# Joining a unit's row maxima at the start of a step, and storing 18 units' maxima transposed by element-wise DMAs

## The chip, the cores and the metric

The kernel runs on one core of one Trainium2 chip. A core has a matrix engine (TensorE, PE in the profile, with its weight loads shown as PEld), a vector engine (VectorE, DVE), a scalar engine (ScalarE, ACT), a general engine (GpSimd, POOL), and a queue engine (SyncE, SP) that here does nothing but issue DMAs. The engines run side by side, each through its own instructions in program order, and wait for one another by semaphores. The metric is the device time of one execution in microseconds (us); lower is better.

## The reference

The input x has 2048 tokens of 512 features. It is normalised (layernorm without weights), and two branches read the result. One is an attention with 32 heads of 16 features; the other is an MLP with a hidden width of 1376. The output is x plus the attention's result times the silu of the MLP's result.

```
xn = layernorm(x)
q, k, v = split(xn @ wqkv)                      # 32 heads of 16
p = softmax(q @ k.T / 4, over the keys)
s = concat_heads(p @ v) @ wo
g = silu(gelu(xn @ w1 + b1) @ w2 + b2)
out = x + s * g
```

The softmax needs, for every query and head, the largest score over the 2048 keys. It is subtracted before the exponential. The change is about how these maxima get from the engine that finds them to the place where they are subtracted.

## The kernel before

The attention is cut into 32 units. A unit is 4 heads times 512 queries: `GH = 4`, `CH = 512`, so `NU = 32`. A unit is worked on twice.

First the maxima. The scores are computed with queries on the 128 partitions ("S tiles", line 185): 64 tiles of 128 queries by 512 keys for a unit. For each tile VectorE takes the maxima of its two halves (`s_max`, line 191) into the unit's tile `mx`. When all 64 are done, `s_end0` joins them: one `tensor_reduce` (line 249) turns 128x128 numbers into 128x16, negated, the tile `nm` (16 is 4 heads times 4 blocks of 128 queries). GpSimd splits it into a high and a low part, the tile `nmh` (`two`, lines 252 and 253). These two are put off to the next "X" place of the order below.

Second the exponentials. The scores are computed again, transposed, with the keys on the partitions ("T tiles", line 713, four for every block of 128 keys, one a head). The negated maxima are two more rows of the query operand `qt`, which the matmul adds to the scores, so that ScalarE can take the exponential of a T tile straight from PSUM (line 715). The probabilities times the values are summed by TensorE into `pv` (line 778); at a unit's end VectorE copies `pv` to `os` (line 785), and DMAs carry it on (`o_move`, `o_den`).

For that second pass the maxima must stand as rows, with the queries along the free side, and not spread over partitions as `nm` has them. In the kernel before, this turn is made by TensorE. `s_end1` (line 269) multiplies `nmh` by an identity into a PSUM tile, which it takes from the same ring of four banks that the T tiles use (`t_tile`); `s_end2` copies it to `mh` (VectorE, line 279; ScalarE, line 277, in the first stage) and stores it by one DMA to the DRAM tensor `mh_d` (line 280). Later `load_mh` (line 153) reads it into the rows of `qt`. The units below `PAIRED = 28` share this step two by two: `nmh` holds 64 columns, and the step is made once for units 0 and 1, once for 2 and 3, and so on, some `tick`s after the second unit of the pair has ended (`later`, `flush`).

The order of all this is written out by hand. In a first stage (up to about 465 us) the MLP and the projections fill TensorE, and the S tiles of units 0 to 8 are put between them by `fill`. Then comes the main loop, 512 steps of 16 per unit, numbered n; `ka` is the step's place in its unit. A step has the four T tiles of one block of 128 keys, the `pv` matmuls of the step before, and three S tiles for later units:

```
ORDER = {0: "TTTTV", 3: "TSXTTSTYV"}
AFTER = {0: "STXTTSTYV", 2: "XTSTTYSTV"}
```

T is one T tile with its exponential, S an S tile with its reduce, X and Y are the halves of a third S tile, V the four groups of `pv` matmuls. Each V also counts `later` down and calls `flush`. With three of 64 tiles a step, a unit of maxima takes 21.3 steps, while a unit of exponentials takes 16, so the maxima start 9 units ahead and the ends of the units of maxima fall on a repeating set of three places `ka` = 6, 11 and 1. In the kernel before, `s_end0` is called inside `s_max` right after the reduce of the next S tile, wherever in a step that is. It also issues on SP the six loads of the query operand for two units later (`load_qs`).

SP takes DMAs in program order. In each unit of the main loop it issues the loads of `qt` (`load_qt`, at step 2) and of its maxima rows (`load_mh`), `o_move` (step 1), the store and reload of the denominators (`o_den`, step 9), and the six loads of `load_qs`. `o_den` begins with a reciprocal on VectorE (line 806) that reads what `o_move` brought; GpSimd divides by the reloaded denominators at step 15 (`o_div`, line 816).

Of the kernel before, what the change touches and what calls it, by code (L numbers as in the profile page):

```python
# [8 lines left out]
F32 = mybir.dt.float32  # L9
# [7 lines left out]
P = 128  # L17
# [7 lines left out]
NCH = S // CH  # L25
# [7 lines left out]
LEAD = 144  # L33
# [8 lines left out]
AFTER = {0: "STXTTSTYV", 2: "XTSTTYSTV"}  # L42
HC = CH // 2
PAIRED = 28
KB = 3
XB = 6
BANKS = ("ttvt", "xtmt", "ttvt")
# [3 lines left out]
def fused(ctx: ExitStack, tc: tile.TileContext, x, wqk, wv, wo, w1, b1, w2, b2, out):  # L51
    nc = tc.nc
# [15 lines left out]
    mh_d = dpool.tile([NG * NCH, 2, GH, CH], F32, name="mh_d")  # L68
# [18 lines left out]
    QS, QT, MX, NM, MH = {}, {}, {}, {}, {}  # L87
    SYNC = mybir.DependencyInfo(mybir.DependencyClass.Sync, mybir.DependencyReason.DATA)
    qss = []
    NU = NG * NCH  # L90
# [13 lines left out]
    def load_k(g, pieces=range(6), eng=nc.sync, c0=0, n=S):  # L104
        both = kws[g % KB]
        for i in pieces:
            a, b = divmod(i, 3)
            r, cs = slice(64 * a + DH * b, 64 * a + DH * b + DH), slice(c0, c0 + n)
            src = rows((qk_h, qk_h, qk_l)[b], g, 1, a, c0, n)
            if both is not None:  # L110
                eng.dma_start(both[r, :, cs].bitcast(F32), src)
            else:
                for p in range(2):
                    eng.dma_start(kts[g % KB][p][r, cs].bitcast(F32), src[:, p])

# [12 lines left out]
    def slot(i, shape, dtype=F32):  # L128
        return big.tile(list(shape), dtype, name=f"slot{i}")
# [8 lines left out]
    def load_qs(u, sides=range(2)):  # L138
        if u < NU:
            QS[u] = qzs[u % 2] if u < LEAD // 16 else qss[0][:, u % 2]  # L140
            q_rows(QS[u], u, sides)

    def ask_qs(u):
        errands[:0] = [(load_qs, u, (a,)) for a in range(2)]
# [11 lines left out]
    made = [0, 0]  # L156
    done = {u: 0 for u in range(NU)}
    later, ended, errands, sent = [], [], [], set()

    def units_of(u):  # L160
        return (u,) if u >= PAIRED else (u - u % 2, u - u % 2 + 1)

    def tick():
        for e in later:
            e[0] -= 1
# [8 lines left out]
    def at_of(job):  # L174
        u, st, p = job
        return divmod(st, NCH) if u % (NCH * KB) else divmod(st, NCH)[::-1]

    def s_mm(ps, job, a, c0, k0, w):
        u, st, p = job
        qi, ki = at_of(job)  # L180
        if u not in MX:
# [3 lines left out]
        return nc.tensor.matmul(ps[:, c0:c0 + w], QS[u][r, p, qi * P:(qi + 1) * P],  # L185
                                kts[u // NCH % KB][p][r, k0:k0 + w], start=True, stop=True).ins

    def s_max(ps, job, heads, parts):
        u, p = job[0], job[2]
        qi, ki = at_of(job)  # L190
        nc.vector.tensor_reduce(MX[u][:, 2 * p:2 * p + 2, qi, ki][:, heads, parts], ps.rearrange("p (n c) -> p n c", c=HC), axis=AX.X, op=OP.max)  # L191
        done[u] += 1
        if ended:
            s_end0(ended.pop())
        if done[u] == 64:
            ended.append(u)
        if done[NU - 1] == 64:
            s_end0(ended.pop())

    def s_whole(job, a):  # L200
        ps = s_tile()[0]
        s_mm(ps, job, a, 0, 0, CH)
        s_max(ps, job, a, slice(0, 2))

    def s_one(a):
        made[a] += 1
        s_whole(heads[made[a] - 1], a)
# [28 lines left out]
    def run_off():  # L236
        while put_off:
            put_off.pop(0)()

    def s_end0(u):  # L240
        nm = qring.tile([P, GH * NCH], F32, name="nm")
        n = len(units_of(u))
        if u == units_of(u)[0]:
            NM[u] = qring.tile([P, 2, 2, GH * NCH], F32R, name="nmh")[:, :n]
        hl = NM[units_of(u)[0]][:, u % n]
        if u == units_of(u)[-1]:
            later.append([12 if "seen" in prog else 8, units_of(u)[0]])
        mx = MX.pop(u).rearrange("p a b c n -> p (a b) (c n)")
        nc.vector.tensor_reduce(nm, mx, axis=AX.X, op=OP.max, negate=True)  # L249

        def two():
            nc.gpsimd.tensor_copy(hl[:, 0], nm)  # L252
            nc.gpsimd.tensor_sub(hl[:, 1], nm, hl[:, 0].bitcast(F32))

        put_off.append(two)
        if "seen" in prog or u == NU - 1:
            run_off()
        del QS[u]
        if "seen" in prog:
            ask_qs(u + 2)  # L260
        else:
            load_qs(u + 2)

    prog = {}

    def s_end1(u):
        pm = s_tile()[0] if "seen" in prog or u == NU - 1 else t_tile()
        n = 2 * GH * NCH * len(units_of(u))
        nc.tensor.matmul(pm[:n, :P], NM.pop(u).rearrange("p u i a -> p (u i a)"), ident_r, start=True, stop=True)
        MH[u] = pm  # L270
# [44 lines left out]
    for j in range(len(pairs)):  # L315
        for h in range(2):
# [4 lines left out]
            due = next((i for i in range(j, len(pairs)) if is_m[i]), len(pairs))  # L321
            nxt = next((i for i in range(j + h, len(pairs)) if is_m[i]), len(pairs))
            left = 2 * (nxt - j) + 1 - h
            need = 4 * sum(is_m[:nxt]) - 4 - nd
            room = 2 * (due + 1 - j) - h
            n = 2 if nd < len(parts) and parts[nd][2] and ready - nd > room else 1
            n = max(n, need - 2 * (left - 1))
# [234 lines left out]
    def fill(a):  # L562
        due = 2 * FILL0 + APART * (put[0] + sum(made))
        if sum(made) < 4 * LEAD and row[0] >= due and (made[0] <= made[1]) == (a == 0):
            taken()
            if later and later[0][0] <= 0:
                put[0] += 1
                u = later.pop(0)[1]
                s_end1(u)
                s_end2(u)  # L570
                return
            s_one(a)
            tick()

    def taken():
        prog["pe"] += 1
        s_when.append(prog["pe"])
        if len(s_when) > 2:
            prog["seen"] = max(prog["seen"], s_when[-3])
# [81 lines left out]
    def errand():  # L661
        if errands:
            f, *args = errands.pop(0)
            f(*args)
# [41 lines left out]
    def t_one(u, k, p, a):  # L706
        g = u // NCH
        if (u, k) not in PT:
            PT[u, k] = slot(3 + len(PN) % 3, (P, GH, CH))
            PN.append(1)  # L710
        ps = t_tile()
        r = slice(64 * a, 64 * a + 3 * DH + 2)
        nc.tensor.matmul(ps, kts[g % KB][p][r, k * P:(k + 1) * P],  # L713
                         QT[u][r, p, :], start=True, stop=True)
        nc.scalar.activation(PT[u, k][:, 2 * p + a, :], ps, AF.Exp, scale=SCALE)  # L715
# [27 lines left out]
            load_mh(0)  # L743
    while errands:
        errand()
    del prog["seen"]
    s_ring.append(ps_x)
    qz.close()
# [71 lines left out]
    def home(i):  # L820
        if i not in homes:
            homes[i] = (slot(i, (P, KT, D)) if i < KB else
                        keep_r.tile([P, 2 * KT, D], F32, name="kt0"))
# [98 lines left out]
    def at(n, f, *a, pos=3):  # L922
        todo.setdefault((n, pos), []).append((f, a))

    KS = tuple(range(KT))
    L = 16 * NU

    def due(n):
        return min(4 * L, 4 * LEAD + max(0, 3 * n - 1))

    for u in range(NU):
        g, c = divmod(u, NCH)
        if c == 0 and g == KB:
            for i in range(6):
                at(56 + i, load_k, g, (i,), nc.gpsimd, 0, S // 2)
                at(64 + i, load_k, g, (i,), nc.gpsimd, S // 2, S // 2)
        elif c == 0 and g > KB:
            for i in range(6):
                at(64 * (g - KB + 1) + 6 + i, load_k, g, (i,), nc.gpsimd)
        if u >= 2:  # L940
            at(16 * u - 14, load_qt, u)
            need = min(n for n in range(L) if due(n) >= 64 * (units_of(u)[-1] + 1)) + (4 if u < NU - 1 else 2)
            at(max(16 * u - 14, need), load_mh, u)
        if u < NU - 1:
            at(16 * u + 17, o_move, u, pos=0)
            at(16 * u + (25 if u < NU - 2 else 19), o_den, u, pos=0)
            at(16 * u + (31 if u < NU - 2 else 22), o_div, u, nc.gpsimd)
    T3 = range(NT - NCH, NT)
    late = range(NW, NT)
    for t in range(NW):  # L950
        n = DONE + 4 * (t // 2)
# [9 lines left out]
    for i, t in enumerate(late):  # L961
        n = L - 2 * len(late) - 1 + 2 * i
# [4 lines left out]
    for k in range(KT):  # L967
        at(104 + 16 * k, load_wo, k)
        at(110 + 16 * k, wo_high, k)
        at(114 + 16 * k, wo_low, k)  # L970
    jobs.extend(heads[made[0]:])
    for n in range(L + 1):
        ua, ka = divmod(n, 16)
        want = due(n) - due(n - 1)
        i = 0
        order = ORDER[want] if n > 1 else ("TTTTV", "TTSTSVT")[n]
        if want == 3 and ua:
            order = AFTER.get(ka, order)
        for op in order:
            if op in "SXY":  # L980
                s_op(op)
            elif op == "V":
                if n:
                    pv_step(*divmod(n - 1, 16))
                for _ in range(4):
                    tick()
                flush()
            else:
                if EARLY <= 4 * n + i < 4 * L:
                    t_one(ua, ka, i % 2, 1 - i // 2)  # L990
                for f, args in todo.get((n, i), []):
                    f(*args)
                i += 1
# [54 lines left out]
```

## Time and profile before

| What | Value |
|---|---|
| median of 3 runs | 1567.34 us (1567.28 to 1567.35) |
| the profiled execution's own time | 1567.11 us |
| its span in the profile | 1565.3 us |
| granted TensorE clock | 1.0 |
| DVE busy | 1418.3 us (91%) |
| ACT busy | 1233.9 us (79%), 9 tenths or more from slice 13 on |
| joins of a unit's maxima (line 249) | 32 of 276 ns |
| turns on TensorE (line 269), copies of them (lines 277, 279) | 18 and 18 |

The profile gives one execution. Busy shares are means over stages with different limits: the first 465 us are the MLP's, the rest is the main loop and a short tail. In a list of groups a row reads: line, engine, operation, output from input, shape, count, then busy time, mean length of one, and the idle time in front. In a timeline a row has its start and length in us, the engine, the line, and in square brackets how long the engine had stood idle and what ended that. In a table of windows a row gives a stretch of time, its length, the busy time and number of instructions of each engine, the granted clock, the busy share of the DMA engines, and GB/s.

### The profile page before, as it was taken

To read this page: it belongs to the slowest core of one execution; us is meant where nothing else is said; L and a number is where in the kernel's file an instruction comes from. 1 tells how busy PE (TensorE), PEld (TensorE's weight loads), DVE (VectorE), ACT (ScalarE), POOL (GpSimd) and SP (SyncE) were. 2 spreads that over 40 slices of the span, in tenths; PEclk is the share of its full clock that TensorE was granted. 3 is DMA by queue.
4 is the path that set the end of the run, shared out by engine and by line. 5 is a ranking of instruction groups with operands and counts; after the bars stand their busy time and mean duration, and the time that the engine had idled before them with its cause. 6 is when DMAs were issued, how large, how long until landed. Compare 5 with 4: busy or idle time off the path is not lost.

```text
span 1565.3 us, 31851 instructions
## 1 busy us (share of the span) xinstructions
PE 1558.7 (100%) x12264; PEld 947.5 (61%) x12264; DVE 1418.3 (91%) x2290; ACT 1233.9 (79%) x2397; POOL 372.1 (24%) x394
## 2 busy tenths in 40 slices
PE   9999999999999999999999999999999999999998
PEld 8888899999994444444444444444444444444455
DVE  7599999999999999999999999999999999999834
ACT  4333333434339999999999999999999999999984
POOL 4145575756640011001000100100000000000043
PEclk9999999999999999999999999999999999999999
DMA  6626343454322113112411511421151111110163
GB/s 209 152 60 155 118 139 99 152 148 135 123 90 62 40 41 61 29 38 46 79 31 28 70 40 33 57 45 29 30 75 28 33 29 33 40 30 22 46 198 113
DMA packets 74647, 116.87 MB, mean 75 GB/s; under 512 B 23012, under 2 KB 24292, under 8 KB 73320
## 3 DMA queue, kind: packets, MB, share of 16 engines
q1 hardware_dynamic: 70748, 101.89, 23.8%
q0 software_dynamic: 3264, 12.35, 4.7%
q8 instruction: 97, 1.59, 0.4%
q10 hardware_dynamic: 484, 0.60, 0.1%
q14 instruction: 54, 0.44, 0.1%
HBM read 84.35 MB, written 25.97 MB: 70 GB/s over the span
## 4 chain that ended last, share of the span: by engine, by line
PE 99%; DVE 1%; ACT 0%; issue 0%; POOL 0%; DVEq 0%; POOLq 0%
PE pv L778 33%; PE pst L713 20%; PE ps L587 13%; PE ps L185 11%; PE pst L587 7%; PE ps L713 6%; PE pv L587 2%; PE ps L902 1%; PE ps L82 1%; PE ps L460 1%; PE pst L82 1%; PE pv L493 1%; PE pst L442 0%; PE pst L460 0%; ACT slot L715 0%
## 5 line engine op out<-in xcount | busy, mean ns | idle before, releaser
L191 DVE TENSOR_REDUCE mx<-ps 128x2 f32<-128x512 f32 x2048 | 1319.9, 687 | 86.3 <-PE ps L185 42.5
L715 ACT ACTIVATE slot<-pst 128x512 f32<-128x512 f32 x1533 | 825.4, 602 | 13.8 <-PE pst L713 6.9
L778 PE MATMUL pv<-slot,vsb 128*32 128x512 f32 x4096 | 545.3, 605 | 0.2 <-DVE os L785 0.2
L713 PE MATMUL pst<-qt,kt 50*128 50x512 f32 x1149 | 380.4, 430 | 0.5 <-DVE gt L646 0.3
L185 PE MATMUL ps<-kt,slot 48*128 48x512 f32 (+1 forms) x1364 | 377.1, 367 | 0.0
L713 PEld LDWEIGHTS pst<-qt,kt 50*128 50x128 f32 x1149 | 191.6, 184 | 256.7 <-ACT slot L715 240.4
L715 ACT ACTIVATE slot<-ps 128x512 f32<-128x512 f32 x515 | 310.4, 603 | 1.9 <-PE ps L185 0.8
L185 PEld LDWEIGHTS ps<-kt,slot 48*128 48x128 f32 x1364 | 225.6, 184 | 40.4 <-DVE mx L191 35.2
L587 PE MATMUL ps<-slot,w1h 64*128 64x512 f32 x1088 | 218.0, 393 | 0.0
L185 PE MATMUL ps<-kt,qz 48*128 48x512 f32 x512 | 201.7, 394 | 0.0
L185 PE MATMUL ps<-slot,slot 48*128 48x512 f32 (+1 forms) x598 | 165.7, 367 | 0.0
L713 PE MATMUL ps<-qt,kt 50*128 50x512 f32 x387 | 159.8, 415 | 0.0
L587 PEld LDWEIGHTS ps<-slot,w1h 64*128 64x128 f32 x1088 | 150.8, 185 | 11.6
L587 PE MATMUL ps<-slot,w1l 64*128 64x512 f32 x544 | 148.2, 392 | 0.0
L778 PEld LDWEIGHTS pv<-slot,vsb 128*32 128x32 f32 x4096 | 80.7, 108 | 100.2 <-issue 92.0
L379 POOL TENSOR_TENSOR hl<-hg,hh 128x512 fp32r<-128x512 f32 x76 | 96.9, 1297 | 151.6 <-ACT hh L378 110.3
L372 ACT ACTIVATE hg<-ps,b_sb 128x512 f32<-128x512 f32 x44 | 27.9, 685 | 125.0 <-PE ps L587 102.1
L252 POOL CAST nmh<-nm 128x16 fp32r<-128x16 f32 x32 | 6.4, 199 | 482.8 <-DVE nm L249 460.2
L713 PE MATMUL pst<-qt,slot 50*128 50x512 f32 x384 | 111.2, 415 | 0.0
L185 PEld LDWEIGHTS ps<-slot,slot 48*128 48x128 f32 x598 | 98.8, 184 | 17.0 <-DVE mx L191 15.1
L185 PEld LDWEIGHTS ps<-kt,qz 48*128 48x128 f32 x512 | 93.7, 183 | 0.4
L713 PEld LDWEIGHTS ps<-qt,kt 50*128 50x128 f32 x387 | 71.1, 184 | 37.5 <-ACT slot L715 31.9
(165 smaller groups left out, 1722.8 us busy)
## 6 DMA issues: line engine op xcount, KB each, us to landing
raw<-in_w SPq DMA_DIRECT2D x88, 256.0 KB
qk_h<-hh SPq DMA_DIRECT2D x32, 256.0 KB
qk_l<-hl SPq DMA_DIRECT2D x32, 256.0 KB
qt<-qk_h SPq DMA_DIRECT2D x128, 64.0 KB
slot<-qk_h SPq DMA_DIRECT2D x92, 64.0 KB
g_d<-gt POOLq DMA_DIRECT2D x16, 256.0 KB, 3.5
qt<-qk_l SPq DMA_DIRECT2D x64, 64.0 KB
dn<-den_d SPq DMA_DIRECT2D x32, 128.0 KB
```

What stands on the lines that cost most here:

```text
L82: nc.tensor.matmul(ps, lhs[a], rhs[b], start=first and n == 0, stop=last and n == 2)
L185: return nc.tensor.matmul(ps[:, c0:c0 + w], QS[u][r, p, qi * P:(qi + 1) * P], kts[u // NCH % KB][p][r, k0:k0 + w], start=True, stop=True).ins
L191: nc.vector.tensor_reduce(MX[u][:, 2 * p:2 * p + 2, qi, ki][:, heads, parts], ps.rearrange("p (n c) -> p n c", c=HC), axis=AX.X, op=OP.max)
L372: nc.scalar.activation(raw, ph.pop(u), AF.Gelu_apprx_tanh, bias=b1_sb[:, u[2]:u[2] + 1])
L379: nc.gpsimd.tensor_sub(hl, raw, hh.bitcast(F32))
L460: nc.tensor.matmul(pq["q", g, c], W1[g][i][:, k * P:(k + 1) * P], (xh, xl)[j][c][:, k], start=n == 0 and k == 0, stop=n == 2 and k == KT - 1)
L493: nc.tensor.matmul(pw[:, :P], ident, ident, start=True, stop=True)
L587: i = nc.tensor.matmul(ps, lhs[r], rhs[r], start=first, stop=last).ins
L713: nc.tensor.matmul(ps, kts[g % KB][p][r, k * P:(k + 1) * P], QT[u][r, p, :], start=True, stop=True)
L715: nc.scalar.activation(PT[u, k][:, 2 * p + a, :], ps, AF.Exp, scale=SCALE)
L778: nc.tensor.matmul(PV[u][32 * j:32 * j + 32, :], vsb[:, k, h:h + 32], PT[u, k][:, j, :], start=(k == 0), stop=(k == NT - 1))
L902: HALF[0] = nc.tensor.matmul(PW[i][0], OTS[i, k][x][r], (wo_h, wo_l)[y][r, k], start=k == 0 and side == 0 and n == 0, stop=k == KT - 1 and ...
```

## The change

`units_of` now pairs only units 0 to 9 (`BYDMA = 10`). Three things differ.

First, the place of the join. `s_max` no longer calls `s_end0`, except for the last unit. In the main loop, ahead of a step's first tile, `s_end0` is called for a unit whose 64 tiles are done: for units 28 and up at the first such place, for the others only when `ka` is over 2 and one further step has passed. In the first stage `fill` calls it after the next S tile, which is where it was.

Second, the turn for units 10 to 27. Their `s_end0` does not put the unit on `later`, so there is no TensorE transpose, no PSUM tile, no copy and no row-wise store. It puts four pieces on the list `pieces`, and in every odd step, at the second T tile, `s_piece` issues one of them on SP: a DMA from `nmh` straight to `mh_d`, for one of the parts (high, low) and two of the four heads. It reads 128 partitions of 8 numbers and writes each number to its own place, 128 numbers apart from the next of its partition, so every piece of 4 bytes is a transfer of its own: 1024 a DMA, spread over 16 DMA engines, 4096 a unit.

Third, the earliest step for `load_mh` is 18 steps after the unit's last tile for units 10 to 27 and 9 for units below, where it was 4 after the pair's.

```diff
 PAIRED = 28
+BYDMA = 10
...
     def units_of(u):
-        return (u,) if u >= PAIRED else (u - u % 2, u - u % 2 + 1)
+        return (u,) if u >= BYDMA else (u - u % 2, u - u % 2 + 1)
...
         done[u] += 1
-        if ended:
-            s_end0(ended.pop())
         if done[u] == 64:
             ended.append(u)
-        if done[NU - 1] == 64:
-            s_end0(ended.pop())
+            if u == NU - 1:
+                s_end0(u)
...
     def s_end0(u):
+        ended.remove(u)
         nm = qring.tile([P, GH * NCH], F32, name="nm")
...
-        if u == units_of(u)[-1]:
+        if BYDMA <= u < PAIRED:
+            pieces.extend((u, i, p) for i in range(2) for p in range(2))
+        elif u == units_of(u)[-1]:
             later.append([12 if "seen" in prog else 8, units_of(u)[0]])
...
-    prog = {}
+    prog, pieces = {}, []
+
+    def s_piece():
+        u, i, p = pieces.pop(0)
+        cs = slice(2 * NCH * p, 2 * NCH * (p + 1))
+        nc.sync.dma_start(mh_d[u, i, 2 * p:2 * p + 2].rearrange("a (q s) -> s (a q)", s=P),
+                          NM[u][:, 0, i, cs].bitcast(F32))
+        if (i, p) == (1, 1):
+            del NM[u]
+            sent.add(u)
...
+            whole_units = list(ended)
             s_one(a)
+            for u in whole_units:
+                s_end0(u)
             tick()
...
-            need = min(n for n in range(L) if due(n) >= 64 * (units_of(u)[-1] + 1)) + (4 if u < NU - 1 else 2)
+            need = min(n for n in range(L) if due(n) >= 64 * (units_of(u)[-1] + 1)) + (9 if u < BYDMA else 18 if u < PAIRED else 4 if u < NU - 1 else 2)
             at(max(16 * u - 14, need), load_mh, u)
...
+    since = {}
     for n in range(L + 1):
...
+        for u in list(ended):
+            if u >= PAIRED or ka > 2 and since.setdefault(u, n) < n:
+                s_end0(u)
         order = ORDER[want] if n > 1 else ("TTTTV", "TTSTSVT")[n]
...
                     t_one(ua, ka, i % 2, 1 - i // 2)
+                if i == 1 and n % 2 and pieces:
+                    s_piece()
```

More of the change, by code (lines that the diff above doesn't have):

```diff
@@ L745, in fused @@
         errand()
+    assert sum(made) == 4 * LEAD
     del prog["seen"]
```

## The prediction

> **What bounds the kernel now.** I read the page first, to see which engine is full where the change acts.
>
> ```profile
> span 1565.3 us, 31851 instructions
> PE   9999999999999999999999999999999999999998
> DVE  7599999999999999999999999999999999999834
> ACT  4333333434339999999999999999999999999984
> q1 hardware_dynamic: 70748, 101.89, 23.8%
> ```
>
> From slice 13 on PE, DVE and ACT are all at nine tenths, so no share of busy time tells what an edit is worth. The main loop is periodic, however: every unit has the same 16 steps, so the length of a unit is the price list. I cut the main loop at the copies of `pv` to `os` (line 785), one a unit, and asked for a table of these windows. The rows below are a choice, and the last is 24 such windows in one.
>
> ```profile
> 536.47:569.39 32.92, 32.92 (x258) 15.40 (x258) 31.04 (x53) 32.66 (x65) 1.66 (x3) 1.00 0.13 34
> 569.39:602.13 32.74, 32.74 (x258) 15.40 (x256) 30.86 (x51) 32.60 (x65) 5.88 (x10) 1.00 0.31 57
> 602.13:635.23 33.10, 33.10 (x259) 15.60 (x259) 31.32 (x54) 32.67 (x65) 3.21 (x6) 1.00 0.28 48
> 635.23:667.98 32.75, 32.75 (x258) 15.45 (x257) 31.02 (x52) 32.63 (x65) 1.70 (x3) 1.00 0.14 35
> 667.98:701.12 33.14, 33.14 (x259) 15.55 (x257) 31.32 (x53) 32.64 (x65) 3.55 (x5) 1.00 0.16 43
> 701.12:733.87 32.75, 32.75 (x258) 15.45 (x256) 30.87 (x52) 32.60 (x65) 3.18 (x3) 1.00 0.12 31
> 733.87:766.79 32.92, 32.92 (x258) 15.41 (x257) 31.02 (x53) 32.65 (x65) 6.15 (x11) 1.00 0.63 90
> 766.79:799.84 33.05, 33.05 (x259) 15.62 (x257) 31.24 (x54) 32.69 (x65) 4.04 (x6) 1.00 0.16 43
> 898.64:931.41 32.77, 32.77 (x258) 15.47 (x256) 31.01 (x53) 32.61 (x65) 1.70 (x3) 1.00 0.12 34
> 1326.53:1359.64 33.11, 33.11 (x259) 15.54 (x258) 31.32 (x54) 32.66 (x65) 1.66 (x3) 1.00 0.13 34
> 536.47:1326.53 790.06, 790.06 (x6155) 371.78 (x6155) 746.05 (x1229) 783.38 (x1537) 66.80 (x110) 1.00 0.22 43
> ```
>
> Two of these windows hold no end of a unit of maxima, 569.39 and 701.12: 32.74 and 32.75 us, 2.05 a step. The others hold a join, or a join with the turn of a pair, and are up to 0.39 longer. To see which place costs what, I looked at three of them in the timeline of DVE, and at the turn on PE: the copy of `pv` and, later in the same unit, a join at the end of a step (first fence), a join in the middle (second), and a turn after a join (third).
>
> ```profile
> 635.23 0.68 DVE L785 COPY os<-pv 128x512 f32<-128x512 f32 x1
> 635.83 3.76 DVE L191 TENSOR_REDUCE mx<-ps 128x2 f32<-128x512 f32 x6
> 639.75 3.90 DVE L191 TENSOR_REDUCE mx<-ps 128x2 f32<-128x512 f32 x6 [0.17 <-PE ps L185]
> 643.82 3.91 DVE L191 TENSOR_REDUCE mx<-ps 128x2 f32<-128x512 f32 x6 [0.17 <-PE ps L185]
> 647.64 0.28 DVE L249 TENSOR_REDUCE nm<-mx 128x16 f32<-128x128 f32 x1
> 647.89 3.91 DVE L191 TENSOR_REDUCE mx<-ps 128x2 f32<-128x512 f32 x6
> 651.72 0.24 DVE L806 RECIPROCAL dr<-dr 128x16 f32<-128x16 f32 x1
> ```
>
> ```profile
> 559.92 0.28 DVE L249 TENSOR_REDUCE nm<-mx 128x16 f32<-128x128 f32 x1
> 560.11 3.16 DVE L191 TENSOR_REDUCE mx<-ps 128x2 f32<-128x512 f32 x5
> 563.55 2.70 DVE L191 TENSOR_REDUCE mx<-ps 128x2 f32<-128x512 f32 x4 [0.28 <-PE ps L185]
> ```
>
> ```profile
> 608.27 0.13 PEld L269 LDWEIGHTS pst<-ident_r,nmh 128*64 128x64 f32 x1 [0.84 <-issue]
> 608.27 0.27 PE L269 MATMUL pst<-ident_r,nmh 128*64 128x128 f32 x1
> 608.59 0.28 DVE L279 COPY mh<-pst 64x128 f32<-64x128 f32 x1
> 609.04 3.31 DVE L191 TENSOR_REDUCE mx<-ps 128x2 f32<-128x512 f32 x5 [0.17 <-PE ps L185]
> ```
>
> In an ordinary stretch DVE stands idle some 0.17 us ahead of a step's first reduce, for TensorE is then at the `pv` matmuls and has no new S tile. The join at 647.64 falls into just this gap: the next reduce starts 0.25 later, which is the gap and the overlap of two reduces, and its window (635.23) is 32.75, no longer than an empty one. The join at 559.92 stands between two reduces of one step: it pushes the rest of the step back, TensorE gets its S banks back later, DVE then waits 0.28 for it, and the window (536.47) is 32.92, 0.17 longer.
>
> **The change part by part.**
>
> *The join moves* for 18 units, 10 to 27. Their ends come in a cycle of three. Those of 12, 15, 18, 21, 24 and 27 stand at a step's end already; they move one step on (`ka` 8), gain nothing, and cost what windows 635.23 and 898.64 show: 0.00 to 0.02. The reciprocal, at present two steps behind the join (651.72), is then one step behind; every step has its own gap again, so nothing adds up. The other 12 stand in the middle of a step, at 0.17 each (536.47 and 733.87, 32.92 against 32.75). They move to `ka` 13 and `ka` 4. At 13 nothing is near. At 4 the copy of `pv` (0.68 us, at the end of `ka` 0) lies behind: it is part of every window, so its cost is in the 32.75, and its lag is over when DVE has its gap of 0.17 again, at 639.75, the start of `ka` 3, a step before the join. I take 0.01 for the new place, from between 635.23 and 898.64. Below nothing is excluded, as a window can't fall under the empty one by taking no work out; the upper end is the present 0.17. Gain 12 x 0.16 = 1.9.
>
> *The turn goes* for 9 pairs: a weight load, a matmul of 0.27, a PSUM bank out of the T tiles' ring, and a DVE copy of 0.28 that cannot start before the matmul. Its price is a window with the turn less one with the same join alone: 33.10 - 32.92 = 0.18 (602.13), 33.14 - 32.92 = 0.22 (667.98), 33.05 - 32.75 = 0.30 (766.79), three pairs of each sort: 3 x 0.70 = 2.1.
>
> The sum over all is checked by the long window: 790.06 - 24 x 32.75 = 4.06, against 12 x 0.17 + 2.1 = 4.14. I take 4.06, less 18 x 0.01 for the joins at their new places: 3.9.
>
> *Units 28 and up* keep the turn. Unit 28's join goes to a step's start, so window 1326.53 should go from 33.11 to the 33.05 of a turn behind such a join: 0.06, rounded up to 0.1 with unit 8, whose join leaves the first steps of the loop. Unit 29's goes to `ka` 2, where the copy of `pv` still leaves no gap (635.83 to 639.75); it gains nothing, and I leave it at 0.
>
> *GpSimd* has the same two instructions a unit, a step or more later for most. Nobody on the path waits for them now; the first piece on SP does. Queued behind that piece on SP are loads with many steps to spare: `load_qs` is issued ahead of the pieces and serves a unit that starts 17 steps or more later.
>
> *SP* gets 72 DMAs for 9. The trace has no DMA of 4-byte pieces. For the issue and the transfer I have these rows:
>
> ```profile
> L280 SPq DMA_DIRECT2D mh_d<-mh x18: 313/518/535, 158.1 to 1486.4; - x18
> L153 SPq DMA_DIRECT2D qt<-mh_d x64: 587/660/745, 452.5 to 1488.6; - x64
> SPq L798 <- DVE mx L191: 374.4, 30, 21.4
> SPq L810 <- DMA den_d<-dr: 50.0, 32, 7.0
> ```
>
> An issue takes 0.31 to 0.75 us here whatever is moved; were it by the row (0.518 for 64), 1024 would take 8.3. I take 0.75, the longest seen: 3 us a unit. SP waits 374.4 / 30 = 12.5 us in each unit at `o_move` alone, so it has the room; at 8.3, four pieces are 33 us of the 21.3 x 2.05 = 43.7 between two ends, and SP would run late. The transfer: the queue's 70748 packets took 23.8% of 16 engines' span, 0.238 x 16 x 1565.3 / 70748 = 84 ns each, most of them far larger than 4 bytes. A piece puts 64 on each engine: 5.4 us. From below, the wait for a store of 128 rows of 64 bytes is 50.0 / 32 = 1.6 us; if all of it went by the row, eight times as many would take 12.5. Between 1.6 and 12.5 I take 5.4, the row with most packets behind it. Four are 22 us of each 43.7, side by side with the loop: 0 on the path. That other traffic costs the loop nothing is seen in 733.87 against 536.47: the DMA engines 63% and 13% busy, both 32.92.
>
> *`load_mh`* is put later for units 26 and 27 alone; for unit 27 from step 418 to 424, with need at 432. Its last piece is issued at step 415, so it has 8 steps, 16 us, for what now takes two issues of 0.66 and a landing. 0.
>
> In sum 3.9 + 0.1 = 4.0 us. The profiled execution took 1567.11, of which 1.8 lie outside its span; it stands 0.23 under the median. So 1567.34 - 4.0 = 1563.3, that is 0.26% faster.
>
> **The rivals.** *Half of it.* The join costs as much at its new place, or what the turn held up is late for another reason next. Without the first term 1567.3 - 2.0 = 1565.3, without the second 1565.4. For it speaks that the gap (0.17, and 0.25 between two starts) has no room to spare beside a join that takes 0.25, and that at `ka` 4 the gap has been back for one step only. Against it: two windows with a join in the gap, 0.00 and 0.02.
>
> *The pieces do not drain: slower.* The place is SP's queue. The other transfers fill 0.13 of the DMA engines in an ordinary window, 5.7 of 43.7 us, so the point is (43.7 - 5.7) / 4 = 9.5 us a piece, 148 ns a packet. Beyond it every unit is late by more, and in the end `load_mh` and the T tiles behind it wait. At 12.5 us a piece: first join 559.9, 18 x (50 + 5.7) later is 1563, while unit 27's T tiles start about when the copy at 1359.64 is made; some 200 us late, 1770 in all. Just past the point it is a few us to tens. For it speaks that no row prices a 4-byte write to DRAM; against it the 84 ns, which are a mean over mostly larger pieces. The Trainium skill speaks for this rival: "DMA: Bandwidth & Descriptors", section "Rules for kernel authors", says that a last dimension that isn't contiguous becomes one descriptor for each element, and that a transpose by such a pattern is 19 times dearer than the hardware's. No run here shows that ratio; as an estimate by that page, 19 times the 0.518 us of the old store is 10 us a pair, of 87, and would still drain.
>
> *It does nothing.* If ScalarE's own pace set the step, the extra time would only move. But its share is not full in any window (32.60 of 32.74, 32.64 of 33.14), and the windows with turns are longer for the same 65 exponentials.
>
> **How the numbers follow.** Forecast 0.66, half 0.20 (with "nothing" in it), slower 0.14, in which 0.08 is the queue at its point and 0.06 a smaller wait at SP or DVE that I don't see. This kernel's measurements tell about 0.2%, 3.1 us, from no change: the forecast is past it (1563.3 is 0.8 below 1564.2), half is not. The forecast's own range is 1562.7 to 1564.2: downward 0.3 at unit 8 and 0.3 if the rotation of the T tiles' banks, shifted by 9 turns, helps the tail, upward 18 x 0.05. The range asked for takes in half and stops short of the queue: 1562.5 to 1566.3.
>
> **What would show it.** Windows from 536 to 1326 all at 32.74 to 32.80, their sum near 786; the turn's instructions on TensorE 9 in place of 18; DVE's idle time ahead of a first reduce gone where a join is, and nowhere a join between two reduces of a step. It is wrong if windows with a join at `ka` 4 or 13 stay at 32.9, if a piece is over 9.5 us from issue to landing, or if DVE waits at the reciprocal or `os` for a DMA.

## The result, and the profile after

The changed kernel takes 1588.0 us, the median of runs from 1585.3 to 1591.0, against 1567.3 (1567.2 to 1567.4) for the kernel before: a ratio of 1.0134, interval 1.0122 to 1.0146, so 20.7 us slower, where 4.0 us faster was forecast. The profiled execution is the shortest of these runs, 1585.32 us. From the page, its span, engines and DMA queue:

```profile
span 1583.4 us, 31943 instructions
PE   9999999999999999999999999999999999999999
DVE  7599999999999999899999988999999999999834
ACT  4323333333449999899999999999999999999984
q1 hardware_dynamic: 144908, 101.89, 31.4%
```

The page hardly shows it. The engines stay at eight and nine tenths, and the queue moves the same 101.89 MB in twice the packets: 74160 more, close to 72 x 1024. The windows between two copies of `pv` to `os` (line 800 now) do show it; the columns are those of the prediction's table, and the last row is all 24 windows that were 790.06 before:

```profile
536.47:569.25 32.78, 32.78 (x258) 15.46 (x258) 31.05 (x53) 32.65 (x65) 1.67 (x3) 1.00 0.17 35
569.25:602.42 33.17, 33.04 (x258) 15.45 (x258) 30.88 (x51) 32.65 (x65) 3.04 (x6) 1.00 0.49 46
602.42:635.18 32.76, 32.76 (x258) 15.51 (x258) 31.00 (x52) 32.65 (x65) 4.70 (x9) 1.00 0.48 59
635.18:672.31 37.13, 33.79 (x260) 15.70 (x259) 31.10 (x53) 32.76 (x65) 2.95 (x4) 1.00 0.30 31
672.31:705.06 32.75, 32.75 (x258) 15.47 (x256) 31.04 (x52) 32.58 (x65) 3.53 (x5) 1.00 0.20 42
805.35:839.81 34.46, 33.98 (x258) 15.43 (x257) 31.04 (x52) 32.81 (x65) 4.17 (x5) 1.00 0.38 33
872.93:905.69 32.76, 32.76 (x258) 15.54 (x256) 30.98 (x53) 32.56 (x65) 7.54 (x15) 1.00 0.74 78
939.12:976.28 37.16, 35.05 (x256) 15.96 (x255) 31.28 (x52) 32.50 (x64) 2.99 (x4) 0.95 0.31 31
1042.36:1077.23 34.87, 33.91 (x258) 15.58 (x256) 31.29 (x52) 32.87 (x65) 2.68 (x4) 1.00 0.44 36
1343.67:1378.10 34.43, 33.77 (x259) 15.63 (x257) 31.41 (x53) 32.69 (x65) 1.66 (x3) 1.00 0.17 34
536.47:1343.67 807.20, 798.48 (x6146) 374.30 (x6146) 744.09 (x1220) 784.43 (x1537) 66.43 (x110) 1.00 0.37 42
```

Two things stand in this table. Windows such as 536.47, 602.42, 672.31 and 872.93 are 32.75 to 32.78, which is what was forecast for all of them: there the join costs 0.00 to 0.03, and there is no turn. Others are up to 4.4 us longer, irregularly, and in the longest of them TensorE itself is idle: 3.34 us in 635.18, where it was never idle in a window before. The timeline of that window around the hole:

```profile
635.78 1.88 DVE L192 TENSOR_REDUCE mx<-ps 128x2 f32<-128x512 f32 x3
...
636.87 0.62 ACT L729 ACTIVATE slot<-ps 128x512 f32<-128x512 f32 x1
...
637.30 0.55 PE L727 MATMUL pst<-qt,kt 50*128 50x512 f32 x2
...
639.75 0.18 PEld L186 LDWEIGHTS ps<-kt,slot 48*128 48x128 f32 x1 [2.34 <-remote]
...
639.77 1.57 ACT L729 ACTIVATE slot<-pst 128x512 f32<-128x512 f32 x3 [2.27 <-remote]
639.80 1.89 DVE L192 TENSOR_REDUCE mx<-ps 128x2 f32<-128x512 f32 x3 [2.14 <-remote]
```

ScalarE ends its work at 637.49, VectorE at 637.66, and TensorE its T matmuls at 637.85 (the ends of matmuls are modelled in the profile). ScalarE has only to read that tile and VectorE the S tile beside it, yet both start at 639.8, within 0.05 us of TensorE's next weight load. So by the profile no engine is waiting for the work of another here: the work is done, and the word of it does not arrive. In the trace's list of semaphore updates, engines' and DMAs' alike, there is none from 637.09 to 639.60, and then they come in a burst some 10 ns apart. Data still move in that time: between 637.1 and 639.6 the trace has 227 DMA packets. I call such a stretch a gap, and counted gaps of over 0.6 us between 500 and 1480 us, and beside them when the first and the last of a store's 16 completions arrive after its issue (medians over all stores):

```
kernel           gaps   sum us   longest us   store's first / last completion, us
before              0      0        0.43        -
changed            52     60.9      2.79       9.2 / 21.0
```

The gaps are where the long windows are. Of the 24 windows 5 hold no gap, and these are 32.75 to 32.78; 19 hold one or more, and 18 of these are 32.94 to 37.16. The one left is 872.93, whose two gaps of under 1 us cost nothing.

The store itself had looked cheap at its issue, and so it is on SP. Rows of the store and of the reads by `load_mh`, then of the turn, then of SP's waits, all of the changed kernel:

```profile
L271 SPq DMA_DIRECT2D mh_d<-nmh x72: 376/527/1996, 561.7 to 1332.6; - x72
L154 SPq DMA_DIRECT2D qt<-mh_d x64: 587/659/756, 452.3 to 1507.1; - x64
```

```profile
L280 PE MATMUL ps<-ident_r,nmh x6: 246/275/277, 157.3 to 1502.6; 128*64 128x128 f32 x5, 128*32 128x128 f32 x1
L280 PE MATMUL pst<-ident_r,nmh x3: 247/248/248, 1371.5 to 1460.3; 128*32 128x128 f32 x3
```

```profile
SPq L825 <- DMA den_d<-dr: 131.9, 32, 11.0
SPq L154 <- DMA mh_d<-nmh: 28.9, 4, 8.1
SPq L137 <- DMA mh_d<-nmh: 25.5, 12, 5.8
```

An issue has a median of 0.53 us and the turns are 9. But the wait of SP for the small store of the denominators, which shares nothing with the maxima, rose from 50.0 us over 32 times to 131.9 (it is 66.6 in the run of the whole change without this layout, below): the word of other DMAs comes late too.

### The profile page after: what moved, and what is told of

Its sections match the earlier page's. It is cut to its first block, busy times and chain, and to the rows that moved or that the text cites. A ratio compares the mean times of both kernels' runs of the same rounds, so it can differ in the third digit from the quotient of the medians.

```text
span 1583.4 us, 31943 instructions
## 1 busy us (share of the span) xinstructions
PE 1567.7 (99%) x12255; PEld 952.1 (60%) x12255; DVE 1416.0 (89%) x2281; ACT 1234.5 (78%) x2397; POOL 371.4 (23%) x394
## 3 DMA queue, kind: packets, MB, share of 16 engines
q1 hardware_dynamic: 144908, 101.89, 31.4%
## 4 chain that ended last, share of the span: by engine, by line
PE 98%; DVE 1%; issue 0%; ACT 0%; another core or an unknown queue 0%; POOL 0%; DVEq 0%; POOLq 0%
PE pv L793 32%; PE pst L727 21%; PE ps L601 12%; PE ps L186 12%; PE pst L601 7%; PE ps L727 5%; PE pv L601 2%; PE ps L917 1%; PE ps L83 1%; PE ps L471 1%; PE pst L83 1%; PE pv L504 1%; DVE mx L192 0%; PE pst L453 0%; PE pst L471 0%
## 5 line engine op out<-in xcount | busy, mean ns | idle before, releaser
L729 ACT ACTIVATE slot<-pst 128x512 f32<-128x512 f32 x1533 | 810.4, 600 | 24.5 <-PE pst L727 7.1
L186 PE MATMUL ps<-kt,slot 48*128 48x512 f32 (+1 forms) x1364 | 382.6, 370 | 7.6 <-remote 1.9
L727 PE MATMUL pst<-qt,kt 50*128 50x512 f32 x1149 | 341.7, 426 | 0.5 <-DVE gt L660 0.3
L729 ACT ACTIVATE slot<-ps 128x512 f32<-128x512 f32 x515 | 316.3, 615 | 8.9 <-PE ps L727 6.4
L727 PE MATMUL ps<-qt,kt 50*128 50x512 f32 x387 | 166.5, 432 | 0.0
L727 PEld LDWEIGHTS pst<-qt,slot 50*128 50x128 f32 x384 | 61.3, 185 | 99.5 <-ACT slot L729 88.0
L831 POOL TENSOR_TENSOR ot<-ot,dn 64x512 f32<-64x512 f32 x15 | 19.1, 1276 | 382.4 <-DMA dn<-den_d 240.1
```

The source lines that it names most:

```text
L727: nc.tensor.matmul(ps, kts[g % KB][p][r, k * P:(k + 1) * P], QT[u][r, p, :], start=True, stop=True)
L831: eng.tensor_mul(ot[c][rs, g // 2], ot[c][rs, g // 2], DN.pop(u)[rs])
```

## The experiments

The kernels of the first four runs were timed beside a kernel before of 1566.99 us, the next four beside 1566.82, the last three beside 1566.75. Counts of gaps are as above.

**The joins alone.** Kernel before with the joins at their new places; pairs, turns and row-wise stores stay, and the read of a unit's maxima is put off by one step. Of its edit, the lines in `fill`:

```
...
+            whole_units = list(ended)
             s_one(a)
+            for u in whole_units:
+                s_end0(u)
...
```

> The kernel before with the first part of the change alone: the joins at a step's start. Pairs, the turn on TensorE and its row-wise store stay; the maxima rows are loaded one step later. Theory A (the 4-byte stores are what costs, and the joins do what was forecast): 1565.3 us, 2.0 under before, and no stretch without semaphore updates. Rival B (the moved joins, or the loads behind them that SP now issues later, make the stalls): 1575 us or more.

1565.85 us (1565.52 to 1566.45), ratio 0.9993 (0.9984 to 1.0002), no gap. Four windows of it:

```profile
536.01:568.79 32.78, 32.78 (x258) 15.44 (x258) 30.97 (x52) 32.63 (x65) 1.66 (x3) 1.00 0.13 34
601.54:634.54 33.00, 33.00 (x259) 15.55 (x259) 31.19 (x53) 32.71 (x65) 2.72 (x5) 1.00 0.24 49
634.54:667.37 32.83, 32.83 (x258) 15.58 (x258) 30.99 (x52) 32.66 (x65) 1.71 (x3) 1.00 0.13 34
765.92:799.08 33.16, 33.16 (x259) 15.61 (x259) 31.19 (x54) 32.71 (x65) 4.06 (x6) 1.00 0.18 43
```

A window with a moved join and nothing else falls from 32.92 to 32.78, as forecast. One that keeps its turn falls less (33.10 to 33.00) or rises (33.05 to 33.16), and the join now one step ahead of the reciprocal costs 0.08 (32.75 to 32.83). The moved joins are not the loss; alone they gain 1.1 us at the medians, which the interval does not tell from none.

**The stores alone.** The kernel of the first run, with 72 more DMAs of the shape and at the steps of the changed kernel's, from a constant tile into a DRAM tensor that nobody reads.

```
+    dump_d = dpool.tile([32, 2, GH, CH], F32, name="dump_d")
...
+        nc.sync.dma_start(dump_d[u, i, 2 * p:2 * p + 2].rearrange("a (q s) -> s (a q)", s=P), vsb[:, 0, :8])
```

> e1 with the 72 DMAs of 1024 4-byte pieces added at the steps where the changed kernel has them, from a tile that never changes into a DRAM tensor that nobody reads. Nothing of the computation depends on them. Theory A: 1583 to 1592 us, e1 plus the 20 to 25 us that the changed kernel lies above its forecast; stretches of 0.6 us or more without any semaphore update, 4 to 16 us behind a piece. Rival B: as e1. Rival C (the units wait for late maxima, as their stores land late): as e1, for no unit waits for these.

1610.55 us (1608.04 to 1614.41), ratio 1.028 (1.0265 to 1.0294): 44.7 us over the first run. 49 gaps of 66.4 us, the longest 4.25, completions at 9.0 and 21.8. Three of its windows:

```profile
636.91:675.88 38.97, 35.37 (x260) 16.03 (x257) 31.13 (x53) 32.81 (x65) 2.97 (x4) 0.96 0.39 30
1017.27:1050.03 32.76, 32.76 (x258) 15.45 (x258) 31.01 (x53) 32.65 (x65) 4.45 (x9) 1.00 0.63 79
1254.86:1292.88 38.02, 36.38 (x253) 15.97 (x253) 31.03 (x50) 32.49 (x64) 1.29 (x1) 0.91 0.14 20
```

Nobody waits for these stores, no unit is late by them, and the whole loss is there and more: 1583 to 1592 was expected. So it is not maxima that come late, but what the stores do to the rest. That they cost some 20 us more here than in the changed kernel is settled only in part. Between 500 and 1480 us TensorE is idle for 20.1 us here and for 9.4 there. In the longest windows the granted clock is below 1.00 too (0.96 in 636.91, 0.91 in 1254.86): the trace grants half the clock for 27.3 us of that time here and for 3.4 there, in stretches of 3.4 or 6.8 us, most of which begin within 2.1 us of the end of a gap of over 2 us. At half the speed that is at most 13.7 and 1.7 us. The two differences, 10.7 and 12.0, come to about the 20; why the same stores make longer gaps here stays open.

**Which property of the stores it is.** The same kernel, with the destination changed in one way each.

```
32 bytes:   dump_d[u, i, 2 * p:2 * p + 2].rearrange("a (s c) -> (a s) c", c=8)     128 runs of 32 bytes
64 apart:   dump_d = dpool.tile([32, 4, 8, P, 16], F32)  ... [..., 0]               1024 of 4 bytes
16 apart:   dump_d = dpool.tile([32, 4, 8, P, 4], F32)   ... [..., 0]               1024 of 4 bytes
8 apart:    dump_d = dpool.tile([32, 4, 8, P, 2], F32)   ... [..., 0]               1024 of 4 bytes
in SBUF:    dump = keep.tile([P, 2, 16], F32), each partition to its own, 8 apart   1024 of 4 bytes
half:       36 of the 72 DMAs, as in the stores alone
```

> e2 with the same bytes in pieces of 32: 128 a DMA in place of 1024. Theory A: as e1 within 1 us, 1564 to 1566. If it is the number of DMAs or their place on SP that counts, as e2.

> e2 with each 4-byte piece 64 bytes from the next in DRAM, so that no two pieces of a DMA lie within the same 64 bytes. If several engines that write into the same 64 bytes hold each other up: near e1, under 1570 us. If each small write to DRAM is dear whatever its neighbours are: as e2 or slower.

> e2 with the 4-byte pieces of neighbouring partitions 16 bytes apart: four pieces share 64 bytes, where 16 do in e2 and one does in e4. If sharing in any number is dear: between e2 and e4 by the count, 1575 to 1590. If only sharing between partitions served by different DMA engines is dear, and an engine has four neighbouring partitions: as e4, 1566.

> e2 with the same 72 DMAs of 1024 4-byte pieces, but into an SBUF tile, 8 bytes apart. If it is the writing to DRAM: as e1, 1566 within 1 us. If it is the number of 4-byte packets in the DMA engines: as e2, over 1600.

> e2 with two of the four DMAs of each unit, 36 in all. If the price is by the piece: e1 plus half of e2's 44.7 us, 1588 us. If it comes from pieces that queue up behind one another, less than half: under 1580.

> The unread extra stores once more, single numbers 8 bytes apart in DRAM, so that eight of them share 64 bytes, where 16 apart (four share) cost nothing and 4 apart (sixteen share) cost 44.7 us. Theory (numbers that share 64 bytes must come from different DMA engines to collide, and an engine has 4 neighbouring partitions): 1575 to 1590, with stretches without any semaphore update. Rival (an engine has 8 neighbouring partitions, or the limit lies elsewhere): 1566, as with 16 apart.

```
destination        in 64 bytes   us (lowest to highest)        ratio (interval)          gaps  sum us  completions, us
4 apart                16        1610.55 (1608.04-1614.41)   1.0280 (1.0265-1.0294)    49    66.4    9.0 / 21.8
 half of the DMAs      16        1591.51 (1587.43-1597.60)   1.0161 (1.0141-1.0182)    32    38.8    9.3 / 20.3
8 apart                 8        1566.55 (1565.50-1568.32)   1.0000 (0.9991-1.0010)     7     5.7    4.4 / 7.6
16 apart                4        1565.72 (1565.18-1566.07)   0.9993 (0.9984-1.0002)     0      0     3.3 / 5.2
64 apart                1        1566.13 (1565.70-1566.50)   0.9994 (0.9985-1.0003)     0      0     2.6 / 4.1
in SBUF                 -        1566.15 (1565.45-1566.47)   0.9996 (0.9986-1.0005)     0      0     2.2 / 3.2
32-byte runs            2 runs   1566.26 (1565.68-1566.64)   0.9994 (0.9985-1.0003)     0      0     1.4 / 2.7
```

The number of DMAs and their place on SP cost nothing (32-byte runs). 73,728 packets of 4 bytes cost nothing on the path either (64 apart, and in SBUF), nor do they as writes to DRAM. Only where single numbers from different partitions lie next to one another in DRAM do completions take 21 us and semaphore updates stop for long. 16 bytes apart they cost nothing, 8 apart they show the first gaps at a time that the interval does not tell from none, 4 apart they cost 44.7 us, and half as many stores a little over half of it, 25.7. My expectation for 8 apart, 1575 to 1590, was too high; the time of its rival, 1566, came true. I count by 64 bytes, but the runs vary only the spacing, and with it the length of DRAM that a store covers (4 KB at 4 apart, which the 32-byte runs cover too, at no cost). That 64 bytes is the size that matters, and not a smaller or a larger one, they do not show. And the numbers in SBUF lie 8 bytes apart, each in its own partition, so that run shows nothing about neighbours 4 bytes apart in SBUF.

Which engine writes which number the trace does not say. The Trainium skill, "DMA: Bandwidth & Descriptors", section "The descriptor swizzle", gives each engine groups of four neighbouring partitions for a transfer to 128 partitions, on trn2 also for one issued as these are, from SP; stores out of the partitions it does not speak of. If they are split the same way, four numbers to the 64 bytes come from one engine, eight from two and sixteen from four. The runs at 16 and at 4 apart go with engines that get in each other's way; the run at 8 apart, for which that reading asked 1575 or more, does not bear it out. So this stays an assumption. The same page, section "Specifications", says that below 512 bytes a DMA engine reads, modifies and writes. All these stores are far below it, and every layout but the one with sixteen to the 64 bytes costs nothing that can be measured, so by itself that rule does not tell the dear one from the cheap.

**Runs of 16 bytes in the changed kernel.** Partition s of query tile q takes query 4s+q of the unit, so that a partition's four numbers of a head are neighbours in DRAM. The S matmuls then load as weights columns that lie 16 bytes apart.

```
...
+            qs = QS[u][r, p].rearrange("r (s q) -> r q s", q=NCH)[:, qi]
...
+        nc.sync.dma_start(mh_d[u, i, 2 * p:2 * p + 2].rearrange("a (s q) -> s a q", s=P), ...
```

> The changed kernel, with the queries of units 10 to 27 dealt to the partitions of an S tile so that partition s has queries 4s to 4s+3 over the four tiles. The four numbers of a head and partition then are neighbours in DRAM: a DMA has 256 pieces of 16 bytes, and each run of 64 bytes comes from four partitions that follow one another. Same result, same 72 DMAs at the same steps. Theory A (it is the sharing of 64 bytes of DRAM by 4-byte pieces of many partitions): 1563 to 1564 us, what was forecast for the change. Rival C (units wait for late maxima whatever the pieces are): over 1580.

1636.35 us (1636.19 to 1636.45), ratio 1.0444 (1.0430 to 1.0458), with no gap and completions at 1.5 and 3.3, where 1563 to 1564 was expected. The stores are mended, and something else is slower: a window of the loop, and the weight loads of S tiles, the second row those of the first units, which keep neighbouring columns:

```profile
574.01:609.84 35.83, 35.83 (x258) 19.91 (x259) 30.85 (x51) 33.07 (x65) 6.36 (x11) 1.00 0.34 52
```

```profile
L189 PEld LDWEIGHTS ps<-kt,slot x1364: 182/306/329, 609.6 to 1548.9; 48*128 48x128 f32 x195
L189 PEld LDWEIGHTS ps<-kt,qz x512: 182/183/185, 58.6 to 419.7; 48*128 48x128 f32 x171
```

A weight load has a median of 306 ns where it had 183, and every window with these loads is 3.0 us longer. PEld has 19.91 us of loads in place of 15.45 (window 569.25 of the changed kernel), and TensorE is busy to the full.

**All of the change but the layout.** The changed kernel with its stores as 32-byte runs. The maxima of units 10 to 27 so reach the T tiles in another order of queries, and the exponential has 1/1024 of its scale, so the output is not the reference's and only the time counts.

```
-        nc.sync.dma_start(mh_d[u, i, 2 * p:2 * p + 2].rearrange("a (q s) -> s (a q)", s=P),
+        nc.sync.dma_start(mh_d[u, i, 2 * p:2 * p + 2].rearrange("a (s c) -> (a s) c", c=8),
```

> The changed kernel with its 72 stores as runs of 32 bytes in place of single numbers: the number of DMAs, their bytes, their steps, the moved joins and the 9 dropped turns stay as changed. The maxima of units 10 to 27 so reach the T tiles in another order of queries than they should, and the exponential is given 1/1024 of its scale so that it stays finite: the output is not the reference's. Theory (the loss is the 4-byte layout in DRAM alone, and the rest of the change does what the prediction's sum says): 4.0 us under the kernel before, about 1563.0 beside 1567.0; windows of a unit 32.74 to 32.80 throughout, no stretch over 0.6 us without a semaphore update, a store landed 3 us after its issue. Rival (the two terms share their cause, as with the joins alone, which gave 1.1 us of 2.0): 1565 to 1566. Rival (something else in the change stalls the cores too): 1570 and up.

1563.20 us (1562.82 to 1563.64), ratio 0.9977 (0.9969 to 0.9986), no gap, completions at 1.3 and 2.4. Some of its windows, and in the last row the 24 from 536.26 on:

```profile
536.26:569.03 32.77, 32.77 (x258) 15.45 (x258) 31.04 (x53) 32.64 (x65) 1.65 (x3) 1.00 0.13 35
601.78:634.56 32.78, 32.78 (x258) 15.48 (x258) 30.98 (x52) 32.63 (x65) 2.71 (x5) 1.00 0.22 48
634.56:667.38 32.82, 32.82 (x258) 15.60 (x256) 30.99 (x52) 32.62 (x65) 1.70 (x3) 1.00 0.13 35
667.38:700.13 32.75, 32.75 (x258) 15.49 (x258) 31.00 (x53) 32.63 (x65) 3.54 (x5) 1.00 0.15 42
765.64:798.63 32.99, 32.99 (x258) 15.61 (x258) 30.99 (x53) 32.66 (x65) 4.82 (x6) 1.00 0.15 43
1290.39:1323.32 32.93, 32.93 (x258) 15.57 (x256) 31.01 (x53) 32.64 (x65) 1.70 (x3) 1.00 0.13 35
1323.32:1356.39 33.07, 33.07 (x259) 15.57 (x259) 31.31 (x53) 32.64 (x65) 1.66 (x3) 1.00 0.13 35
536.26:1323.32 787.06, 787.06 (x6146) 372.13 (x6146) 743.20 (x1220) 783.39 (x1537) 66.59 (x110) 1.00 0.21 43
```

So everything in the change but where the 4 bytes go gains 3.6 us, and the layout alone loses 24.6 (1.0134 - 0.9977 = 0.0157 of 1567). The other scale is not what gains: ScalarE is busy 783.39 us in the 24 windows, and was 783.38 in the kernel before. The 24 windows of the changed kernel are 20.1 us longer than these, and TensorE is idle for 8.7 of that; the other 11.4 count as busy in its rows, so idle time alone does not give the price of the gaps.

**A version that beats both.** The stores of 16 bytes in the right order, with GpSimd putting the query columns in that order before they are weights: the queries come in two halves through a buffer of 2 KB a partition, and two copies of 48 x 512 follow each. Of its edit, the copy:

```
...
+            nc.gpsimd.tensor_copy(QS[u][r, p].rearrange("r (q s) -> r q s", s=P),
+                                  qraw[r].bitcast(F32).rearrange("r (s q) -> r q s", s=P))
...
```

> The changed kernel with stores of 16-byte runs in the right order: partition s of query tile q holds query 4s+q, and GpSimd puts the columns of the loaded queries in that order (4 copies of 48 x 512 a unit, by way of a buffer of 2 KB a partition, the queries loaded in two halves), so that the weight loads stay contiguous. Theory (single numbers in DRAM are the whole loss, and the slower weight load of the variant with strided columns was its whole loss): the loop as in the run with 32-byte runs, 1563 to 1564. GpSimd's copies cost some 0.6 us each by the row of a 128 x 512 cast (610 ns), 2.4 us a unit beside an engine that is busy 2 to 6 of 32.75 us; no weight load over 190 ns in its median. Rival (GpSimd and VectorE get in each other's way): reduces longer by some per cent in these stretches, up to 0.5 us a unit, 1570. Rival (strided columns were not the cause): 1600 and up again.

1563.21 us (1562.76 to 1563.91), ratio 0.9977 (0.9968 to 0.9986), no gap, completions at 1.5 and 3.2. The copies, the weight loads and the 24 windows:

```profile
L157 POOL CAST slot<-qraw 48x512 fp32r<-48x512 f32 x72 | 82.2, 1142 | 243.7 <-DMA qraw<-qk_h 153.9 <-PE ps L202 38.5 <-PE pst L745 29.6
L202 PEld LDWEIGHTS ps<-kt,slot 48*128 48x128 f32 x1364 | 226.1, 184 | 39.3 <-DVE mx L208 31.3 <-issue 4.2
```

```profile
535.73:1322.49 786.76, 786.76 (x6146) 372.37 (x6144) 743.35 (x1220) 783.37 (x1537) 141.13 (x176) 1.00 0.23 43
```

A copy takes 1142 ns, nearly twice my 0.6, and still costs the loop nothing: VectorE is busy 743.35 us, as in the run before (743.20). With the columns contiguous the load is 184 ns again.

## Why the prediction was wrong

*Bounds of the kernel, the periodic loop:* right. The five of the 24 windows without a gap are 32.75 to 32.78 in the changed kernel.

*The joins, 1.9, and the turn, 2.1, with 0.1 for units 28 and 8:* right in the sum, not in its parts. In the run without the 4-byte layout the windows of the long stretch fell by 790.06 - 787.06 = 3.0 where I had 3.9, and the span by 3.6 (1565.3 to 1561.7) where I had 4.0. That the sum comes so near is partly luck, for 0.6 of it lies outside these windows, where I had 0.1. Two windows are at 32.93 and 32.99, and a join next to the reciprocal costs 0.07 (634.56) where I had 0.02 and said that nothing adds up. The two terms are also not independent: the joins alone give 1.1, because a window that keeps its turn does not get the join's 0.17 back. I had read the turn as the difference of two windows, and that holds only if both edits are made.

*Units 28 and up:* right in kind. The first window with a turn behind an early join is 33.07 in the run without the layout, where I had 33.05.

*SP's issues:* right, 0.53 us in the median where I took 0.75, though the longest is 2.0. What I overlooked is that a piece behind SP's wait at `o_move` waits too. I had the four pieces of a unit two steps apart, 4.1 us. In the changed kernel 26 of the 54 distances between two pieces of a unit are under 1 us and the longest is 19.8; in the run with 32-byte runs it is 32 of 54, and that costs nothing.

*The transfer:* this is the step that failed. "Between 1.6 and 12.5 I take 5.4 ... 0 on the path." The last completion comes 21.0 us after the issue, beyond my upper end, and the term that I put at 0 is 24.6 us: while the stores are on their way, no semaphore update arrives for up to 2.8 us at a time, and the engines stop. With it goes "that other traffic costs the loop nothing": I showed that for large transfers (window 733.87) and carried it to 4-byte writes without a row. The 84 ns a packet were not too low for 4-byte packets as such: 64 apart and in SBUF the last completion comes after 4.1 and 3.2 us, under the 5.4. What no row of before could show was single numbers 4 bytes apart, sixteen in the same 64 bytes.

*The rivals.* "The pieces do not drain" had the right sign and my chance of 0.08, and its falsifying sign came true, a piece of more than 9.5 us from issue to landing. Its mechanism did not: stores overlap in flight, SP's waits for them come to 28.9 + 25.5 us over 16 times, on a queue with room, and unread stores lose more. The loss is at the engines, at places that do not wait for a store. The estimate that the prediction worked out by the Trainium skill ("DMA: Bandwidth & Descriptors", section "Rules for kernel authors"), 10 us a pair by its 19 times, took the issue of the old row-wise store, 0.518 us, for the price of a transfer, and a pair has eight stores in place of one; a single store already takes twice those 10 us, and the same number of packets spread over more DRAM takes a fifth of it. "Half of it" and "does nothing" do not apply.

*What would show it:* the turns are 9, the joins stand between steps, and the windows' sum of 786 was nearly met, at 787.06 and 786.76, in the two runs without the layout.

## What to carry to other kernels

When a store writes single numbers from many partitions, look at how close together they land in DRAM and not at how many there are; give each partition a run of 16 bytes or more, or keep the numbers 16 bytes apart, and price the layout by one unread copy of the store in the loop before building on it. When TensorE, VectorE and ScalarE all stop at one time and start within 0.1 us, with a releaser that had long been done or that is given as remote, look for a stretch in which no semaphore update arrives, and for the transfer issued some 4 to 16 us earlier. A term that is read as the difference of two windows holds for the edits together; one of them alone may give half.

## What the runs showed of the hardware that was not expected

With stores of single numbers 4 bytes apart in DRAM, sixteen to 64 bytes, no semaphore update of the core arrives for up to 2.8 us (changed kernel) and 4.3 us (stores alone), those between TensorE, VectorE and ScalarE included. In the changed kernel these gaps begin 4.3 to 16.1 us after the store last issued, half of them 7.6 to 10.4, and only 26 of the 72 stores are followed by one before the next store is issued. Why these, and how the one leads to the other, no run shows. The loading of weights is slower where the columns lie 16 bytes apart, 306 ns against 183, and this cost 3 us a unit, some 70 us in all, twenty times what the rest of the change gains. And GpSimd can reorder 48 x 512 numbers four times a unit, 4.6 us, without a trace in VectorE's busy time.
